# State part of a gated recurrence in 64-row tiles, with two output banks a chunk and a new hand-set order

## The chip, the cores and the metric

The kernel runs on one core of a Trainium2 chip. The metric is the device time of one execution in microseconds (us), lower is better. The engines are named as the profile names them: PE (matrix products; PEld is its weight load), DVE (vector), ACT (activation), POOL (general) and SP, whose queue issues the DMAs.

## The reference

Two stages follow each other. Per batch (4) and head (8), a recurrence over 768 steps with a 48 x 48 state, which is gated by alpha along its rows:

```python
for t in range(S):
    state = alpha[:, :, t, :, None] * state + np.einsum('bhd,bhe->bhde', k[:, :, t], v[:, :, t])
    y[:, :, t] = np.einsum('bhd,bhde->bhe', q[:, :, t], state)
```

Its output, with the heads side by side as 384 columns, is x. Then a mix over time of rank 32 and an MLP with a hidden width of 1536:

```python
xt = x.transpose(0, 2, 1)
h = xt @ U @ V
u = x + h.transpose(0, 2, 1)
ch = np.maximum(u @ w_ch1, 0.0) @ w_ch2
return u + ch
```

All inputs and the output are float32; the kernel computes its products in bfloat16 with float32 sums.

## The kernel before

**Chunks.** The 768 steps of a batch are cut into six chunks of 128. Inside a chunk the recurrence becomes products of matrices. `lt` is the logarithm of alpha, its cumulative sum over time comes from a product with a triangle of ones (L541 for whole chunks), and its exponentials `aa` and `ai` (L552, L551) scale q and k into `rkq` (L562). Scaled q and k are transposed to `kqt`, either on PE (L576) or, for the six chunks of batch 3, by a DMA that SP issues (L588). Their product gives the scores (L604), which a mask cuts to the past (L614, `pm`). The output of a chunk is y = scores x v (L671) + q x state (L666). The state is carried on: k x v of the chunk (L627) is added to the old state (L654, `sm`) and scaled by the chunk's total decay `tot` (L638, `st`).

**Two kinds of chunk.** In batch 0 and in the first four chunks of batch 1, loads come as pairs: one load holds four heads of two chunks (`stage_pair`). The other fourteen chunks are whole (`stage_gla`): chunks 4 and 5 of batch 1, and all of batches 2 and 3. The change is in the whole chunks. Heads stand there in pairs p = 0..3. In `kqt`, the even head of a pair lies in rows 0 to 47 and the odd one in rows 64 to 111. The score products use this: with `o = 64 * par` they take 48 rows each, in 64-row tiles of the PE array, even heads into one PSUM bank and odd heads into another. The state part of y does not: per pair it is one product over all 128 rows, which gives the 96 columns of both heads. For that the state must be zero where an even head's rows meet an odd head's columns. `tot` does it: it is made by two exponentials (L554), each with a bias from `off` of -30000 in one half of the rows, so that the total is 0 there. All of y of a chunk lies in one bank of 384 columns and is copied to `xb` by one instruction (L273 on ACT, L275 on DVE).

**After the recurrence.** `stage_mix` makes the mix of rank 32 (L686, L716) and the sum `ub` (L717), which is transposed to `uT` on PE (L736), or for batch 3 by DMA (L722). `mlp1` (L767) gives the hidden rows, ACT (L777) and DVE (L779) apply the maximum, `mlp2` (L793) gives the output, DVE adds `ub` (L799), and SP stores it (L802, L804). The 24 weight tiles are loaded once (L305) and cast by POOL or ACT.

**What sets the order.** Nothing is scheduled at run time or by the compiler. `P.add` lists every operation with the engines it may run on; the strings TABLE and SLOTS then say, operation by operation, which comes next, on which engine, and in which buffer of its pool. Each engine works through its instructions in that order. SP's queue does too: a load waits at its head until its buffer (one of 40 named `io`) has been read by the last user, and a store or a transpose by DMA until its data are made. The numbers of nanoseconds in `P.add` are a planner's estimates and do not act at run time. There are eight PSUM banks, given out by SLOTS, and four `kqt` buffers.

Of the kernel before, what the change touches and what calls it, by code (L numbers as in the profile page):

```python
# [16 lines left out]
A8SCcABASCzABQSETACePChACfAA+SCgACjDC1PC4AC3AC2AEVPEYABISA9SCiDCkPCmDClPBBSC5GEXADjADlPDnAEWACnDDmACoPCqDA-SCdGCrPCsDBDS  # L17
C0GDCPBCSC6GC7PBESCvPCpDC8PC+DDKACtPCuDCwPCxDDDDC9AC-PDADDBDABSAFGAGPAHDAJPAKADMPDPABKSCyDDEPDNADGPDFDDqGDsPBJSDpGDrPDtA
DuDDHPDJADZPBYSG2ABSSEaGBHSDLGDoAEcPDyPEeADIDBFSDQGDaPDbDDSPDUDDvPDwDBMSBLSDkGDzPD0DDxDG4PD8AD+PBRSEZGEbPEdDD3PDcPDdDDOA
BGSDRGDTPDVDG5AEAAD1PD2DBUSGfABOSEDGEfPEhDEgDD-AG7ABNSECGEBAG6ABTSBcSEUABPSD9GGhPGiAGjAGkAD4PELPBVSBWSGlGGmGBgSBXSGgGAAS  # L20
ADGBZSG8GAiSAjGAQSAeSAfGAgSAhGDWPDXDEiPD5PD7ABkSD6AEjPEkDEFPEEPEHAHNADYDEGDElPEMPENDAOSAPGARGEmPDfPAMSANGDePEnPEoADgPDiD
DhAAYSAZGBaSG9GAWSAUSAVGEIPEJDEKDHmAHPPHSAEPPGnPAXGASSATGHQABdSHTGBbSG3GEpAHRABiSBfSHOGAaSBhSBeSBoSAcSAkSBlSBjSAmSBpSAoS
BqSBmSGoPGqDGpDEOPAqSBnSHoPHrAEQPESDAuSAsSGuPGvDGwDEqPGrPGtDGsDERAErPHpAHqAHtGE8PE5PAwSAySEwPG+PHADE2PBrSEsAExPEyAE6PE7D
FFPE9PE+DA2SE3PEtPEzPFBPFCDFHPEuPFJPFGDE4AEvAE0PE1AF1PH-AFIDGyPF5PF3PF4DE-PFADFfPFgDF6AF2AFDPFhPFiAGxDFlPFmAFdPA4SACSFED
A0SFKDFLPFMAFNPFODG-PFjPFkAFeDA6SFVPFWAIBPICAFRPFSAHUGHBDHCPHDDAdGBsSGzPIEAIDAHFPFtPHGDHHDHIGIGGG0AAbAFuAHVPHXAG1AFnPHJP
B0SBwSBySB4SB8SFPPBuSBzSFQAHEDHKPHLAHMAHcPHdDHeDHsDIFAIVAFTPFUAFoAFrPFsAFpPHvPFqDHfDHxAHWPIXPIYAHuPHwDFvPFwDFZPFaDFzPF0D
HYAHiPHZPHbDHaDIZAAnAHyPHzDIHDFbPApAFcAHhPFxPFyAFXPHjPHkAHlAFYAHnGH1PH2DH3DH4DIIPIKAH6PAlGIaGIcPIbGIdPIfAIJPArGGTPIeAH7P
GNPH0DH8PH+AILDIMPH9DIODIgPIhDGBPIAGIPPH5GIRDF7PGZPHgGAzGAtAAvAAxAGOPINDITPF8PIQDIiDISGIWAIjPA5GGaPA3AGCPIUAAEGIkAIlPImD
GUPA1GA7AGbPGcDIvPIwDALGIzPI0DI1PI2DF9PF+DItPIuDGDPKLAGPPInPIpPIqDGEDKNPK0AI3PIxPIyDIoDKfAKOAI4AKPAKhPKjAKnGGVPGWDK2PK3A
LJAKlAJfPJgALeAKRAIrPIsDJRPJjPJSAJkDJdPJeAKiAKkAK6AKQAI5PJHPJIDJPPJQAJLPJMAI-PJAAK5AK4ALgPLkAJFPJGDJJPJKDLjABxSKmGKoPKqA  # L30
JTPJUDI6DKTGKVPJnPJoDLiALhABvSKMGBtSKSGKgAKUPJXPKWDKXDKbPKcDJlPLLPLMAJYDJbPJmAB9SB2SK8GKvPJBPK+PKwDKxDLAACASJcDJDPJEAB1S
KpPKrDGQDLOAK7GLNAJCAI9PI+ALPACESK9PK-DCMSNlAI7PI8DJVPJWALzAB3SK1GKsPKuDLBPLDDLCDKYPKZDJvPJNPJOAB6SLRGLTPLVAJhPL1PL2AL3A
B+SCCSB5SLHPLIANnPNqAB-SKtDLfALlGLnPKaDJwPL5GLQDCBSL4GLEPNrAKyPKzAJiAOIAB7SLKALpAGHPJZPGIPLSPLUAJaALFDLGGLmGKBPL6PL8DGJP
L7PGKDL9ALoPLqACNSCISCFSNoANsGLZPLaDJxPJyDNpACGSNtGKCPCKSCLSCQSCUSCDSLWPLXDL+PLrPKdPKeALYDLtDKDPJ7PLuPN2AN4PN5AJ8PJpPLbG
LsDLvDL-DLwGMADL0GOaAOcPOgAOfAOdACHSNmGN3GLcPN6ALdAN+GJ9PLxPLyDKEDMBPJqPNuSNvPNwDMCAMDPJrPOeAGMSNxDJ+DMEAN7AN8AOKPOMAAIG
MTPMUDMNPJ1PMLPMRPKGPMODJsDMMDCSSCRSOhGNyPNzDN0PMHPMIDKHPMFPMGDOsAOuPKIPMPPMQAMSDMJPMKDOOAMVPMWDKJDJ2PCWSOvAOLAMfPMXPMYD
J3PMjPM7POiGCYSO+AGFSCTSGGSPAPN1AONAObGGYSCJSCXSOtGCaSGSSKFSGLSN9GOwACPSOjSCVSOzGO0DOPDMkDMgDOxAOyAPBAPCAMbPMcDMpPMqAMlP
MmAJ4DNBPODPNDPMZPM-POEDMaAM8ANCACOSOQGNADM1PM2AOkPM5PNEDMxPMyAN-SM9PMhPM3PM4AJuSF-SMtPM6AMuAOJGOVPCZSPDGPEDOmDOlDOFDOWD
OXGMdPMeDM+AOnPOoDOpGNFPNGDMnPMoAMvPMiAOqPOrAOAPOBDO1SO2PO3DO4DOCDORSJ-SOSPOUDNHPMrPMsANRPMzPO5PO6DO7GOTDO8PO9ANSPGRSCbS
O-APFSJ5SPGPM0DPIDPHDGXSOGPOHANTPNUDOYPMwANIPPJPPKAOZAGASNJPNbPPLPNMPNcPPMAPPPPQDPSPPXPPNPPODPRSPYDPTDNdPNKDPUPPVDPWSNWP  # L40
# [101 lines left out]
def mm(*cols):  # L142
    return sum(max(c / 2.4 + 2.5, 25.0) for c in cols)
# [3 lines left out]
def kernel(  # L147
# [35 lines left out]
    QUEUE_U = (3,)  # L183
    P = Plan()
# [57 lines left out]
    off = const.tile([C, 2], FP32, name="off")  # L242
    nc.vector.memset(off, 0.0)
    nc.vector.memset(off[64:128, 0:1], -30000.0)
    nc.vector.memset(off[0:64, 1:2], -30000.0)
# [77 lines left out]
    def paired(b, c):  # L323
        return c // 2 < PAIRS[b]
# [22 lines left out]
    def xk(b, xb, c):  # L347
        return [(xb, c, 0), (xb, c, 1)] if paired(b, c) else [(xb, c)]
# [182 lines left out]
    def stage_gla(b, c, sprev, xb):  # L531
# [21 lines left out]
        for two in range(2 if c < NC - 1 else 0):  # L553
            P.add({"ACT": 100}, lambda e, two=two: nc.scalar.activation(  # L554
                tot().rearrange("p (a two) x -> p a (two x)", two=2)[:, :, two], cb()[:, DM : DM + HP], AF.Exp, bias=off[:, two : two + 1]
            ), r=[cb], w=[(tot, two)])
# [63 lines left out]
        if c < NC - 1:  # L620
# [15 lines left out]
            def f_st(e, src):  # L636
                eng = nc.gpsimd if e == "POOL" else nc.vector
                eng.tensor_tensor(  # L638
                    st().rearrange("p a (two d) -> p (a two) d", two=2),
                    src.rearrange("p (a d) -> p a d", d=D),  # L640
                    tot().to_broadcast([128, HP * 2, D]), op=ALU.mult,
                )

            if sprev is None:
                P.add({"DVE": 450}, lambda e: f_st(e, db()[:, 0:DM]), r=[db, (tot, 0), (tot, 1)], w=[st])
            else:
                sm = Buf(sms)
                W = DM // len(sprev)
                for n, (x, at0, key) in enumerate(sprev):

                    def f_add(e, n=n, x=x, at0=at0):
                        cs = slice(n * W, (n + 1) * W)
                        old = x()[:, at0 : at0 + HP // len(sprev), :].rearrange("p a d -> p (a d)")
                        nc.vector.tensor_tensor(sm()[:, cs], db()[:, cs], old, op=ALU.add)  # L654

                    P.add({"DVE": 460 if len(sprev) == 1 else 270}, f_add, r=[db, key], w=[(sm, n)])
                P.add({"POOL": 885, "DVE": 450}, lambda e: f_st(e, sm()), r=[(sm, n) for n in range(len(sprev))] + [(tot, 0), (tot, 1)], w=[st])

        yb = Buf(bank)

        def f_y(e):
            y = yb()[:, 0:DM]
            if sprev is not None:
                for p in range(HP):
                    x, at0, _ = sprev[p * len(sprev) // HP]
                    nc.tensor.matmul(  # L666
                        y[:, 2 * p * D : (2 * p + 2) * D], lhsT=qT()[:, p, :], rhs=x()[:, at0 + p % (HP // len(sprev)), :],
                        start=(p == 0), stop=False,
                    )
            for h in range(H):  # L670
                nc.tensor.matmul(  # L671
                    y[:, h * D : (h + 1) * D], lhsT=pm()[:, h // 2, h % 2, :], rhs=rv()[:, h, :],
                    start=(h == 0 and sprev is None), stop=(h == H - 1),
                )

        P.add({"PE": mm(*([2 * D] * 4 if sprev is not None else []), *[D] * 8)}, f_y, r=[qT, rv, (pm, 0), (pm, 1)] + [x[2] for x in sprev or ()], w=[yb])
        P.add({"ACT": 385, "DVE": 460}, lambda e: copy(e, xb()[:, c, :], yb()[:, 0:DM]), r=[yb], w=[(xb, c)])
        return st

    def stage_mix(b, xb, ub, uT):  # L680
# [17 lines left out]
        if b == 0:  # L698
# [15 lines left out]
        for c in range(NC):  # L714
# [13 lines left out]
            elif c % 2 == 1 and b > 0:  # L728
# [25 lines left out]
    def mlp1(b, uT, h1, tt):  # L754
        for jt in range(NJ):
            hb = Buf(bank)

            if b == 0:
# [99 lines left out]
```

## Time and profile before

| | us |
|---|---|
| median of 3 runs (lowest, highest) | 161.85 (159.73, 162.47) |
| the profiled execution, first to last instruction | 161.6 |
| busy: PE, PEld | 149.2, 98.7 |
| busy: DVE, ACT, POOL | 105.7, 90.8, 66.0 |
| L767 on PE (288 products) | 53.2 |
| L793 on PE (300 products) | 53.1 |
| bytes moved by DMA | 31.05 MB, 192 GB/s |

The span is what the times of all rows refer to: 0 is the first instruction of the program. Busy time of PE counts overlapping products once; a single product lasts longer (326 ns for 384 columns) than the distance from its start to the next one's. So PE's cost is read from start to start, not from the length of one. In rows of the timeline, the numbers are the start and the length of a group of like instructions that follow each other, and what stands in brackets is idle time ahead of it and what ended that. In rows of the grouped view they are busy time, the mean of one instruction in ns, and the idle time before with its releasers. "SPq" is SP's queue at work issuing a DMA.

### The profile page before, as it was taken

The page shows a single profiled execution, that of the slowest core. Times are in us where ns is not written, and L with a number is a line of the kernel's source. Part 1 is how long each engine was busy: PE and PEld are TensorE (multiplying, and loading weights), DVE is VectorE, ACT ScalarE, POOL GpSimd, SP SyncE. Part 2 cuts the span into 40 slices and gives each one's busy share as a digit, 9 for nine tenths or more (in the row PEclk, how much of TensorE's full clock was granted, in tenths as well). Part 3 has the DMA queues.
Part 4 walks back from the last instruction along what each step waited for, and adds up shares of the span by engine and source line. Part 5 has one row for each costly group of instructions (what it writes and reads, how often), then busy time and mean ns, then how long its engine had stood idle before and what let it go on. Part 6 is the DMA issues. An engine that isn't in the chain of part 4 may idle for free.

```text
span 161.6 us, 4518 instructions
## 1 busy us (share of the span) xinstructions
PE 149.2 (92%) x1728; PEld 98.7 (61%) x1728; DVE 105.7 (65%) x232; ACT 90.8 (56%) x234; POOL 66.0 (41%) x104
## 2 busy tenths in 40 slices
PE   0699897999999999999999999999889999999992
PEld 0586675665667656666676666755457565666662
DVE  6269897966697729559975959682898172334143
ACT  4765797557977645996897472845524301445000
POOL 8099756477667340283563664144622000000000
PEclk9999999999999999999999999999999999999999
DMA  4999995999999969889999899999992047840034
GB/s 125 289 312 315 248 250 150 268 336 253 285 229 279 293 130 209 176 176 203 207 195 215 160 189 198 195 226 204 146 204 67 0 81 172 262 146 0 0 129 163
DMA packets 96964, 31.05 MB, mean 192 GB/s; under 512 B 90640, under 2 KB 96912, under 8 KB 96944
## 3 DMA queue, kind: packets, MB, share of 16 engines
q1 hardware_dynamic: 96944, 30.78, 81.2%
q8 instruction: 13, 0.21, 0.5%
q14 instruction: 7, 0.06, 0.1%
HBM read 23.89 MB, written 4.72 MB: 177 GB/s over the span
## 4 chain that ended last, share of the span: by engine, by line
PE 54%; SPq 20%; DMA 14%; issue 4%; POOL 3%; DVE 2%; ACT 1%; POOLq 0%; DVEq 0%
PE ps L793 24%; PE ps L767 19%; SPq L332 13%; DMA io<-in_q_dram 5%; SPq L339 3%; DMA kqt<-rkq 3%; DMA io<-in_moe_w_ch_dram 2%; DMA io<-in_k_dram 2%; DMA io<-in_v_dram 2%; PE ps L576 2%; SPq L802 2%; SPq L305 2%; PE ps L604 1%; PE ps L716 1%; DVE pm L614 1%
## 5 line engine op out<-in xcount | busy, mean ns | idle before, releaser
L767 PE MATMUL ps<-uT,w_sb 128*128 128x384 bf16 x288 | 53.2, 326 | 0.4 <-POOL w_sb L277 0.4
L793 PE MATMUL ps<-w_sb,h1t 128*128 128x384 bf16 (+2 forms) x300 | 53.1, 319 | 0.0
L777 ACT ACTIVATE h1t<-ps 128x384 bf16<-128x384 f32 x61 | 27.6, 497 | 23.2 <-PE ps L767 23.1
L793 PEld LDWEIGHTS <-h1t 128*128 128x128 bf16 x300 | 27.1, 97 | 15.6 <-issue 0.8
L767 PEld LDWEIGHTS <-w_sb 128*128 128x128 bf16 x288 | 26.5, 98 | 16.4 <-POOL w_sb L277 1.2
L779 DVE TENSOR_SCALAR h1t<-ps 128x384 bf16<-128x384 f32 x35 | 18.6, 553 | 14.2 <-PE ps L767 14.2
L799 DVE TENSOR_TENSOR io<-ub,ps 128x384 f32<-128x384 bf16 (+2 forms) x25 | 13.3, 533 | 10.2 <-PE ps L793 10.0
L614 DVE TENSOR_TENSOR pm<-ps,maskc 128x512 bf16<-128x512 f32 x28 | 17.7, 682 | 1.1 <-PE ps L604 1.1
L562 POOL TENSOR_TENSOR rkq<-io,ai 128x384 bf16<-128x384 f32 x12 | 11.4, 949 | 13.8 <-DMA io<-in_k_dram 8.5
L717 DVE TENSOR_TENSOR ub<-xb,ps 128x384 bf16<-128x384 bf16 x24 | 12.4, 548 | 4.5 <-PE ps L716 4.3
L446 DVE TENSOR_TENSOR pm<-ps,maskp 128x512 bf16<-128x512 f32 x20 | 13.1, 683 | 2.4 <-PE ps L435 2.4
L562 POOL TENSOR_TENSOR rkq<-io,aa 128x384 bf16<-128x384 f32 x11 | 10.0, 912 | 9.8 <-ACT aa L552 8.4
L273 ACT CAST xb<-ps 128x192 bf16<-128x192 f32 (+1 forms) x27 | 10.3, 404 | 6.3 <-PE ps L671 4.9
L277 POOL CAST rv<-io 128x384 bf16<-128x384 f32 x18 | 9.4, 529 | 10.3 <-DMA io<-in_v_dram 9.3
L277 POOL CAST w_sb<-io 128x384 bf16<-128x384 f32 x16 | 8.0, 518 | 7.5 <-DMA io<-in_moe_w_ch_dram 7.5
L273 ACT COPY kqt<-ps 128x512 bf16<-128x512 bf16 x17 | 9.8, 610 | 1.9 <-PE ps L576 1.2
L275 DVE COPY kqt<-ps 128x512 bf16<-128x512 bf16 x19 | 7.8, 420 | 4.0 <-PE ps L576 2.2
L551 ACT ACTIVATE ai<-ps 128x384 bf16<-128x384 f32 x14 | 6.9, 498 | 5.5 <-PE ps L543 3.6
L411 PE MATMUL ps<-ident,rkq 128*128 128x128 bf16 x80 | 8.2, 237 | 1.6 <-DVE rkq L393 1.0
L393 POOL TENSOR_TENSOR rkq<-io,ai 128x384 bf16<-128x384 f32 x8 | 7.3, 910 | 5.8 <-DMA io<-in_k_dram 5.8
L638 POOL TENSOR_TENSOR st<-sm,tot 128x384 bf16<-128x384 f32 x7 | 5.8, 829 | 6.6 <-DVE sm L654 6.6
L393 POOL TENSOR_TENSOR rkq<-io,aa 128x384 bf16<-128x384 f32 x9 | 8.2, 910 | 0.6 <-DMA io<-in_q_dram 0.3
(114 smaller groups left out, 217.1 us busy)
## 6 DMA issues: line engine op xcount, KB each, us to landing
io<-in_alpha_dram SPq DMA_DIRECT2D x24, 192.0 KB, 3.8
io<-in_q_dram SPq DMA_DIRECT2D x24, 192.0 KB, 3.7
io<-in_k_dram SPq DMA_DIRECT2D x24, 192.0 KB, 3.7
io<-in_v_dram SPq DMA_DIRECT2D x24, 192.0 KB, 3.8
io<-in_moe_w_ch_dram SPq DMA_DIRECT2D x24, 192.0 KB, 3.9
out_dram<-io SPq DMA_DIRECT2D x13, 192.0 KB, 1.9
out_dram<-io SPq DMA_DIRECT2D x20, 96.0 KB, 2.3
out_dram<-io SPq DMA_DIRECT2D x1, 120.0 KB, 1.7
```

The costliest lines, as they stand in the source:

```text
L273: nc.scalar.copy(dst, src)
L277: nc.gpsimd.tensor_copy(dst, src)
L332: lambda e: nc.sync.dma_start(t().rearrange("p (h j) d -> p h (j d)", j=2), src[b, hs, sl, :].rearrange("h (p j) d -> p h (j d)", j=2)),
L393: eng.tensor_tensor(jh(dst()[:, :, 0:D]), raw(a), jh(x()), op=ALU.mult)
L446: nc.vector.tensor_tensor(dst, s2, maskp.to_broadcast([C, 2, 2, C]), op=ALU.mult)
L562: eng.tensor_tensor(dst()[:, :, 0:D], a(), x(), op=ALU.mult)
L614: nc.vector.tensor_tensor(pm()[:, :, par, :], s2, maskc.to_broadcast([C, HP, C]), op=ALU.mult)
L767: nc.tensor.matmul(hb()[:, 0:TW], lhsT=w1_sb[:, ct, jt * 128 : (jt + 1) * 128], rhs=u_half(uT, ct, tt, b in QUEUE_U), start=(ct == 0), sto ...
L777: nc.scalar.activation(dst, hb()[:, 0:TW], AF.Relu)
L779: nc.vector.tensor_scalar_max(dst, hb()[:, 0:TW], 0.0)
L793: nc.tensor.matmul(hb()[:, 0 : hi - lo], lhsT=h1()[:, jt, c * C : (c + 1) * C], rhs=w2_sb[:, jt, lo:hi], start=(jt == 0), stop=(jt == NJ - 1),
L799: P.add({"DVE": 468}, lambda e, hb=hb, lo=lo, hi=hi: nc.vector.tensor_tensor(flat(ou)[:, lo:hi], ub()[:, c, lo:hi], hb()[:, 0 : hi - lo], ...
```

## The change

For whole chunks:

- The state part of y is its own step `f_ys`. Per pair of heads it has two products of 48 rows and 48 columns in place of one of 128 rows and 96 columns, the even head in the upper 64-row tile and the odd head in the lower one.
- y lies in two banks, one for even and one for odd heads, with 192 columns used in each. Each is copied to `xb` by an instruction of its own, with a target in blocks of 48 columns.
- `tot` is made by one exponential of four columns; `off` and its three fills are gone. The state's blocks between heads of a pair are no longer set to 0, and nothing reads them. The scaling (`f_st`) spreads one factor over 96 columns.
- The order of all operations, the engine of those that may run on several, and the buffers are new (TABLE and SLOTS), for the whole program. `SUM_U` only gives the test for batch 0 a name.

```diff
-        for two in range(2 if c < NC - 1 else 0):
-            P.add({"ACT": 100}, lambda e, two=two: nc.scalar.activation(
-                tot().rearrange("p (a two) x -> p a (two x)", two=2)[:, :, two], cb()[:, DM : DM + HP], AF.Exp, bias=off[:, two : two + 1]
-            ), r=[cb], w=[(tot, two)])
+        if c < NC - 1:
+            P.add({"ACT": 100}, lambda e: nc.scalar.activation(tot()[:, 0:HP, 0], cb()[:, DM : DM + HP], AF.Exp), r=[cb], w=[tot])
...
-        yb = Buf(bank)
+        yb = Buf(bank), Buf(bank)
+
+        def f_ys(e):
+            for p in range(HP):
+                x, at0, _ = sprev[p * len(sprev) // HP]
+                for par in range(2):
+                    o = 64 * par
+                    nc.tensor.matmul(
+                        yb[par]()[:, p * D : (p + 1) * D],
+                        lhsT=qT()[o : o + D, p, :], rhs=x()[o : o + D, at0 + p % (HP // len(sprev)), par * D : (par + 1) * D],
+                        start=(p == 0), stop=False, skip_group_check=True,
+                    )
 
         def f_y(e):
-            y = yb()[:, 0:DM]
-            if sprev is not None:
+            for par in range(2):
                 for p in range(HP):
-                    x, at0, _ = sprev[p * len(sprev) // HP]
                     nc.tensor.matmul(
-                        y[:, 2 * p * D : (2 * p + 2) * D], lhsT=qT()[:, p, :], rhs=x()[:, at0 + p % (HP // len(sprev)), :],
-                        start=(p == 0), stop=False,
+                        yb[par]()[:, p * D : (p + 1) * D], lhsT=pm()[:, p, par, :], rhs=rv()[:, 2 * p + par, :],
+                        start=(p == 0 and sprev is None), stop=(p == HP - 1), skip_group_check=True,
                     )
...
+        if sprev is not None:
+            P.add({"PE": mm(*[D] * 4)}, f_ys, r=[qT] + [x[2] for x in sprev], w=[yb[0], yb[1]], mode="R")
+        P.add({"PE": mm(*[D] * 8)}, f_y, r=[rv, (pm, 0), (pm, 1)], w=[yb[0], yb[1]])
+        for par in range(2):
+            P.add(
+                {"ACT": 250, "DVE": 265},
+                lambda e, par=par: copy(
+                    e, xb()[:, c, :].rearrange("t (p two d) -> t p two d", two=2, d=D)[:, :, par], yb[par]()[:, 0 : HP * D].rearrange("t (p d) -> t p d", d=D)
+                ),
+                r=[yb[par]], w=[(xb, c, par)],
+            )
```

By engine, PE has 48 products more (1776 for 1728), 16 instructions are gone from ACT and DVE has 16 more; POOL and SP have as many as before. In SP's queue the order of loads, transposes and stores is another one: the first load is alpha of batch 1, chunk 4 (a whole chunk) in place of batch 0, chunk 0.

More of the change, by code (lines that the diff above doesn't have):

```diff
@@ L347, in xk @@
     def xk(b, xb, c):
[L348 removed]
+        return [(xb, c, 0), (xb, c, 1)]
     def stage_pair(b, u, sprev, xb):
@@ L656, in stage_gla @@
                     P.add({"DVE": 460 if len(sprev) == 1 else 270}, f_add, r=[db, key], w=[(sm, n)])
-                P.add({"POOL": 885, "DVE": 450}, lambda e: f_st(e, sm()), r=[(sm, n) for n in range(len(sprev))] + [(tot, 0), (tot, 1)], w=[st])
-        yb = Buf(bank)
+                P.add({"POOL": 885, "DVE": 450}, lambda e: f_st(e, sm()), r=[(sm, n) for n in range(len(sprev))] + [tot], w=[st])
+        yb = Buf(bank), Buf(bank)
[9 more added lines that the diff above has]
+                    )
@@ L727, in stage_mix @@
                     )
-            elif c % 2 == 1 and b > 0:
+            elif c % 2 == 1 and b not in SUM_U:
                 ub2 = Buf(bank)
```

93 lines of the change are left out of this document (40 added, 53 removed).

## The prediction

> **What bounds the kernel now.** I read the page's summary first, then windows by stage, then the chain of waits, then the timelines of PE and of SP's queue.
>
> ```profile
> span 161.6 us, 4518 instructions
> ...
> PE   0699897999999999999999999999889999999992
> ...
> DMA  4999995999999969889999899999992047840034
> ```
>
> ```profile
> core 0: us, PE busy (x) PEld busy (x) DVE busy (x) ACT busy (x) POOL busy (x), PEclk, DMA share, GB/s
> 0.00:31.40 31.40, 24.02 (x460) 18.41 (x461) 23.26 (x71) 21.01 (x58) 19.78 (x38) 1.00 0.91 241
> 31.40:60.00 28.60, 27.93 (x360) 17.69 (x358) 19.51 (x42) 20.18 (x51) 18.20 (x31) 1.00 0.99 262
> 60.00:105.00 45.00, 44.93 (x493) 30.41 (x491) 34.62 (x67) 32.29 (x87) 20.26 (x26) 1.00 0.97 193
> 105.00:120.00 15.00, 13.70 (x123) 8.18 (x122) 11.00 (x21) 6.80 (x17) 6.98 (x8) 1.00 1.08 195
> ```
>
> The reader is to see two limits of nearly the same size. PE is full from 31.4 us on, except between 105 and 120 us, where it lacks 1.3 us. The DMA engines are full until about 120 us. No other engine is near its limit in any stage (DVE, the next, has 34.6 of 45 us). The chain says which limit counts where:
>
> ```profile
> 27.58 3.94 DMA io<-in_moe_w_ch_dram
> 32.14 0.50 PE ps L767 x2
> ...
> 114.06 4.30 DMA kqt<-rkq
> 118.41 0.40 PE ps L604 x8
> ...
> 135.20 11.70 PE ps L767 x72
> ...
> 158.73 0.30 DVE io L799
> ```
>
> The MLP starts when its fourth weight tile is there, and the last stop of PE is for a transposed tile of batch 3 at 118.41. From there PE never stops. So the end is the landing of a late transfer plus the PE work that stands behind it, plus 161.6 - 158.7 = 2.9 us of output. A matmul of 384 columns is 11.70 / 72 = 0.1625 us.
>
> **The state part of y.** Row by row on PE, one group between two full-array groups, and the same for y:
>
> ```profile
> 77.19 0.81 PE L767 MATMUL ps<-uT,w_sb 128*128 128x384 bf16 x4
> 77.94 0.84 PE L604 MATMUL ps<-kqt 48*128 48x128 bf16 x24
> 78.71 0.82 PE L793 MATMUL ps<-w_sb,h1t 128*128 128x384 bf16 x4
> 79.37 0.65 PE L767 MATMUL ps<-uT,w_sb 128*128 128x384 bf16 x3
> ```
>
> ```profile
> 55.41 0.33 PE L666 MATMUL ps<-st,kqt 128*128 128x96 bf16 x4
> 55.58 0.36 PE L671 MATMUL ps<-rv,pm 128*128 128x48 bf16 x8
> 55.79 0.81 PE L793 MATMUL ps<-w_sb,h1t 128*128 128x384 bf16 x4
> ```
>
> Read from start to start. The state part (L666) takes 55.58 - 55.41 = 0.17 us; the other eight products (L671) 0.21, so 26 ns for a product of 48 columns. The 24 products in 64-row tiles take 0.77 us, 0.064 for each pair with the changes of shape in it; in turn, at the 55 ns that 128 columns take at the same rate, they would take 1.3. So two row halves run side by side. New, the state part is 4 pairs of 48 columns, 4 x 0.026 = 0.10 us. Twelve whole chunks have a state: 12 x (0.17 - 0.10) = 0.84 us off PE.
>
> Against it: four L767 should take 0.65 and take 0.75 before the tiled group, while four L793 take 0.66 where no shape changes. Entering costs 0.10; 12 pairs at 55 ns are 0.66 of the 0.77, so leaving costs 0.10 too. In PE's order of instructions the shape changes 58 times before and 70 times after, because the new groups stand partly alone: 12 x 0.10 = 1.2 us onto PE. The sum is +0.4 us; were every new group next to another tiled one it would be -0.84, and with the pairs in turn +1.6. I take +0.4. [...]
>
> **Totals, evictions and the second bank.**
>
> ```profile
> L554 ACT ACTIVATE tot<-ps,off 128x4 f32<-128x4 f32 x22 | 5.4, 278 | 0.7 <-POOL st L638 0.7
> L273 ACT CAST xb<-ps 128x384 bf16<-128x384 f32 x13 | 6.2, 482 | 4.9 <-PE ps L671 4.9
> L273 ACT CAST xb<-ps 128x192 bf16<-128x192 f32 x14 | 4.2, 332 | 1.3 <-PE ps L518 1.2
> L275 DVE CAST xb<-ps 128x192 bf16<-128x192 f32 x6 | 2.1, 353 | 0.6 <-PE ps L518 0.6
> L562 POOL TENSOR_TENSOR rkq<-io,ai 128x384 bf16<-128x384 f32 x12 | 11.4, 949 | 13.8 <-DMA io<-in_k_dram 8.5 <-ACT tot L554 2.6 <-ACT ai L551 2.6
> L638 POOL TENSOR_TENSOR st<-sm,tot 128x384 bf16<-128x384 f32 x7 | 5.8, 829 | 6.6 <-DVE sm L654 6.6
> L534 ACT ACTIVATE lt<-io 128x384 bf16<-128x384 f32 x14 | 7.4, 531 | 0.8 <-DMA io<-in_alpha_dram 0.7
> ```
>
> Eleven of the 22 small exponentials go: -11 x 0.278 = -3.1 us of ACT. Fourteen evictions become 28 of half the width: +14 x (2 x 0.332 - 0.482) = +2.5 us (on DVE 0.353 each). In sum nothing; PE's full work hides both, and if it did not, one chunk's y would come 0.2 us later. The strided target of the new evictions is not in the trace: between the 192-wide row and the 384-wide one, +0 to +2.1 us, taken as 0, since the source holds the same 192 elements. The state's scaling keeps its 384 elements, two more of them on POOL: +1.7 us, in its idle time. A second bank for y, with eight banks in all, can make PE wait for an eviction. The largest such wait before is 0.43 us (next fence), so 0 to +0.5; nothing below 0 comes of it. I take 0, as y's banks are emptied sooner in two halves.
>
> **The order.** It is new on all queues. What counts is SP's order against PE's. Counting DMAs along SP's queue and PE instructions in program order, I take for the n-th DMA the issue time of the n-th before, add the landing and the first step after it, and add the PE work that the new order puts behind the instruction that needs it.
>
> ```profile
> 28.53 1.80 SPq L305 DMA_DIRECT2D io<-in_moe_w_ch_dram  x3
> 69.39 0.66 SPq L339 DMA_DIRECT2D io<-in_alpha_dram  x1
> 80.59 0.76 SPq L339 DMA_DIRECT2D io<-in_v_dram  x1
> 96.10 1.31 SPq L339 DMA_DIRECT2D io<-in_alpha_dram  x1
> 107.22 0.59 SPq L339 DMA_DIRECT2D io<-in_k_dram  x1
> ```
>
> ```profile
> io<-in_alpha_dram SPq DMA_DIRECT2D x24, 192.0 KB, 3.8
> io<-in_k_dram SPq DMA_DIRECT2D x24, 192.0 KB, 3.7
> kqt<-rkq SPq DMA_TRANSPOSE x6, 3.8
> ```
>
> These are the 41st to 43rd, the 90th, 101st, 117th and 130th DMA of SP's queue; the first 90 DMAs are in both orders 40 loads of paired chunks, 22 of whole chunks, 24 weight tiles and 4 small ones, so the same bytes. PE work is counted at 0.1625 us for 384 columns, in proportion for fewer, 26 ns at the least, tiled pairs as one, plus 0.10 for each change of shape.
>
> First the method on the kernel before: behind the tiled group at 118.41 stand 39.5 us and 5 changes, so PE ends at 158.4; it ends at 158.7. I add the 0.3 below.
>
> - Start: alpha of a whole chunk is now loaded first and its logarithm is made first; the second load and one ACT step (0.53) later, PE's first matmul comes some 0.5 us after 3.99 (row below). The three memsets that go were done within that. DMA sets the next 30 us, so I count 0, at most +0.5.
> - Start of the MLP: its third weight tile, which completes the first group, is now the 42nd DMA, not the 39th: issued at about 29.4 (the second of three from 28.53) for 27.6, so 34.0 us for 32.1. But the new order puts more of batch 1 ahead of it, and 117.8 us and 34 changes stand behind: 34.0 + 121.2 = 155.2. No limit.
> - Alpha of batch 2, chunk 1 is the 90th DMA (before, the 79th): 69.4 + 3.8 + 0.53 = 73.7. Its cumulative sum has 415 matmuls of 384 columns (67.4) and 15.0 of smaller work behind it, with 21 changes: 73.7 + 82.5 + 2.1 = 158.3.
> - k of batch 2, chunk 4 is the 101st: 80.6 + 3.7 + 0.95 for the product on POOL = 85.2; behind it 71.5 and 17 changes: 158.4.
> - k of batch 3, chunk 0 is the 117th: 96.1 + 3.7 + 0.95 = 100.8; 55.9 and 10 changes: 157.7.
> - k of batch 3, chunk 5 is the 130th (before the 135th, with five stores more ahead): 107.2 + 3.7 + 0.95 + 3.8 for the transpose = 115.7; 39.0 and 5 changes: 155.2.
>
> ```profile
> 3.99 0.48 PE L371 MATMUL ps<-lt,upto 128*128 128x384 bf16 x1 [3.99 <-DVE off L243]
> ...
> 113.91 0.33 PE L627 MATMUL ps<-rv,rkq 128*128 128x96 bf16 x4 [0.43 <-ACT h1t L777]
> ...
> 118.41 0.40 PE L604 MATMUL ps<-kqt 48*128 48x128 bf16 x8 [0.47 <-DMA kqt<-rkq]
> ```
>
> So the late stop goes: the last transposes have 3 us to spare. What is late next is batch 2's loads, at 70 to 85 us, and they give the same end. The sum: 158.4 + 0.3 + 2.9 = 161.6, the time before. Two limits within 0.1 us of each other leave room for small slips, +0.2. The span was 161.6 and the median of the runs 161.85, +0.25. Forecast: 162.0 us, no change that can be measured (2% or 3.2 us, about what a measurement of this kernel tells from none; its own runs go from 159.73 to 162.47). Its own range is 160.6 (y's changes of shape free, -1.2, and no slip) to 163.0 (evictions and bank waits on the path, 0.5 each).
>
> **The rivals.**
>
> *Faster: batch 2's loads come early enough.* SP stood still for buffers in the kernel before:
>
> ```profile
> SPq L305 <- POOL w_sb L277: 3.2, 2, 2.6
> ```
>
> If the new order has no such stop, everything behind it comes up to 3.2 us sooner, and PE's own work, 155.2 + 0.3 from the start of the MLP, becomes the limit: 155.5 + 2.9 + 0.25 = 158.6. For it: PE had only 1.3 us idle after 31.4 us and DMA fell just short. Against it: the DMA row is at 9 throughout, so that a stop of SP is mostly covered by transfers in flight. Chance 0.13.
>
> *Slower: SP is held by batch 1's buffers.* The new order loads batch 2 and the last weight tiles (72nd to 91st DMA) into buffers that hold k and q of batch 1 until POOL has multiplied them, where the order before used from the 77th to the 84th almost only buffers of weight tiles already cast. POOL does each product in 0.95 us and was busy 18.2 of 28.6 us there. If POOL is behind, the load stands at the head of SP's queue, and all that follow wait with it. One such stop cost 2.6 us before and two 3.2. As the limits of batch 2 have no slack, it goes to the end one for one from the first 0.1 us on: 162.0 + 3.2 = 165.2, and with one us more it is plainly past 2%. Chance 0.16.
>
> *The change does not do what it says:* the two row halves of the state part run in turn after all, 12 x 0.10 = +1.2: 163.2. Against it is the row of the tiled scores. Chance 0.05, within 2%.
>
> **How the numbers follow.** Forecast 0.66, faster 0.13, slower 0.16, in turn 0.05. Of the faster case most lies just past 2% and some within, as does the slower: faster by over 2% 0.12, within 2% 0.71, slower 0.17. The range leaves out a tenth at each end: 158.9 to 165.2.
>
> **What would show it.** A state group standing alone between full-array groups takes about 0.30 us from start to start with its two changes, and one next to tiled scores 0.10. The small exponentials are 11. PE loses some 2 us more than before between 40 and 75 us, waiting for the logarithm of alpha of batch 2, and stops no more than half a microsecond between 105 and 125. The 90th DMA is issued near 69.4. The forecast is wrong if that DMA is issued more than 3 us away from there, or if PE stops for a late transpose or an eviction in the last 40 us.

## The result, and the profile after

The changed kernel takes 168.19 us (median of 4 runs, 166.88 to 169.52) against 161.37 for the kernel before beside it (4 runs, 159.73 to 162.47). The ratio is 1.0425, with a 95% interval of 1.0350 to 1.0499: slower. The forecast was 162.0, the range 158.9 to 165.2; the time lies above both.

The page's summary of the kernel after:

```profile
span 167.1 us, 4594 instructions
...
PE   0589999999869999999899999999999999999991
...
DMA  5999999999999979999999999989970066840153
```

The windows by stage:

```profile
core 0: us, PE busy (x) PEld busy (x) DVE busy (x) ACT busy (x) POOL busy (x), PEclk, DMA share, GB/s
0.00:31.40 31.40, 24.05 (x434) 18.32 (x434) 20.45 (x61) 20.76 (x55) 21.22 (x39) 1.00 1.02 229
31.40:60.00 28.60, 26.47 (x380) 16.84 (x377) 23.16 (x53) 20.48 (x52) 17.38 (x29) 1.00 0.99 240
60.00:105.00 45.00, 43.99 (x476) 29.09 (x474) 33.05 (x64) 26.93 (x73) 16.71 (x23) 1.00 1.14 199
105.00:120.00 15.00, 14.70 (x143) 9.44 (x141) 13.97 (x28) 7.57 (x19) 8.97 (x12) 1.00 0.98 170
```

The late stop is gone, as forecast: between 105 and 120 us PE is busy 14.70 of 15 us, where it was 13.70. The time is lost earlier. From 31.4 to 60 us PE lacks 2.1 us (before 0.7), from 60 to 105 another 1.0 (before 0.1), and in the first 31.4 us it has done 434 products where it had done 460. The chain of waits (start, length, what) has a weight tile and then loads of batch 1 and 2 in these places, and the loads of batch 1 and 2 are long (4.4 to 5.5 us):

```profile
30.40 2.98 DMA io<-in_moe_w_ch_dram
...
33.92 5.54 DMA io<-in_q_dram
...
42.00 5.53 DMA io<-in_q_dram
...
74.23 4.40 DMA io<-in_k_dram
...
78.79 0.91 POOL rkq L558
...
80.34 4.57 DMA io<-in_q_dram
```

What the forecast had not reckoned with is in the DMA view. Here is the same stretch, 6 to 20 us, of the kernel before and of the changed kernel, in this order; in the second line stand packets, MB, and their time as a share of 16 engines:

```profile
DMA packets 10826, 4.13 MB, mean 295 GB/s; under 512 B 10793, under 2 KB 10793, under 8 KB 10825
...
q1 hardware_dynamic: 10825, 4.11, 109.6%
```

```profile
DMA packets 9102, 3.49 MB, mean 249 GB/s; under 512 B 9069, under 2 KB 9069, under 8 KB 9101
...
q1 hardware_dynamic: 9101, 3.47, 120.4%
```

Both kernels load paired chunks there. A packet is the unit that the DMA view counts; here it has 384 bytes, but for a few. Per packet, before took 14 us x 16 engines x 1.096 / 10825 = 22.7 ns, and after 14 x 16 x 1.204 / 9101 = 29.6 ns. The DMA engines are no less full than before and move 16% less. On the page, the median from issue to landing rises for alpha from 3.8 to 4.2 us and for k from 3.7 to 4.5:

```profile
io<-in_alpha_dram SPq DMA_DIRECT2D x24, 192.0 KB, 4.2
...
io<-in_k_dram SPq DMA_DIRECT2D x24, 192.0 KB, 4.5
```

Neither profile says what makes a packet take 29.6 ns in place of 22.7. So the question was what in the change does.

### The profile page after: what moved, and what is told of

Same layout as the page of the kernel before. It is cut to its first block, busy times and chain, and to the rows that moved or that the text cites. A ratio compares the mean times of both kernels' runs of the same rounds, so it can differ in the third digit from the quotient of the medians.

```text
span 167.1 us, 4594 instructions
## 1 busy us (share of the span) xinstructions
PE 152.8 (91%) x1776; PEld 100.6 (60%) x1776; DVE 112.7 (67%) x248; ACT 84.9 (51%) x218; POOL 66.1 (40%) x104
## 4 chain that ended last, share of the span: by engine, by line
PE 52%; SPq 17%; DMA 16%; DVE 4%; POOL 3%; issue 3%; ACT 2%; DVEq 0%; POOLq 0%
PE ps L798 23%; PE ps L772 18%; SPq L330 15%; DMA io<-in_q_dram 9%; DMA io<-in_moe_w_ch_dram 4%; DMA io<-in_k_dram 3%; PE ps L667 2%; PE ps L721 2%; PE ps L600 2%; POOL rkq L558 1%; PE ps L741 1%; POOL rkq L391 1%; PE ps L658 1%; DVE h1t L784 1%; DVE io L804 1%
## 5 line engine op out<-in xcount | busy, mean ns | idle before, releaser
L782 ACT ACTIVATE h1t<-ps 128x384 bf16<-128x384 f32 x54 | 25.6, 492 | 25.8 <-PE ps L772 25.4
L784 DVE TENSOR_SCALAR h1t<-ps 128x384 bf16<-128x384 f32 x42 | 22.1, 550 | 15.7 <-PE ps L772 15.3
L558 POOL TENSOR_TENSOR rkq<-io,ai 128x384 bf16<-128x384 f32 x9 | 8.2, 913 | 16.7 <-DMA io<-in_q_dram 7.6
L271 ACT CAST xb<-ps 128x192 bf16<-128x192 f32 x28 | 8.2, 327 | 11.5 <-PE ps L667 10.1
L558 POOL TENSOR_TENSOR rkq<-io,aa 128x384 bf16<-128x384 f32 x11 | 10.7, 972 | 5.5 <-DMA io<-in_q_dram 2.9
L634 POOL TENSOR_TENSOR st<-sm,tot 128x384 bf16<-128x384 f32 x9 | 7.8, 861 | 10.5 <-DVE sm L646 9.9
L532 ACT ACTIVATE lt<-io 128x384 bf16<-128x384 f32 x14 | 7.4, 528 | 7.1 <-DMA io<-in_alpha_dram 7.1
L275 POOL CAST rv<-io 128x384 bf16<-128x384 f32 x14 | 7.1, 504 | 9.6 <-DMA io<-in_v_dram 8.5
L271 ACT COPY kqt<-ps 128x512 bf16<-128x512 bf16 x15 | 8.8, 592 | 2.9 <-PE ps L572 2.1
L369 PE MATMUL ps<-lt,upto 128*128 128x384 bf16 x10 | 4.3, 432 | 6.3 <-ACT lt L360 6.3
L391 POOL TENSOR_TENSOR rkq<-io,aa 128x384 bf16<-128x384 f32 x10 | 9.1, 913 | 1.7 <-DMA io<-in_q_dram 1.1
```

Source lines behind the costliest of these rows:

```text
L271: nc.scalar.copy(dst, src)
L275: nc.gpsimd.tensor_copy(dst, src)
L558: eng.tensor_tensor(dst()[:, :, 0:D], a(), x(), op=ALU.mult)
L782: nc.scalar.activation(dst, hb()[:, 0:TW], AF.Relu)
L784: nc.vector.tensor_scalar_max(dst, hb()[:, 0:TW], 0.0)
```

## The experiments

### First: the order or the arithmetic?

Two theories were open. O: the new order is slower. A: the new arithmetic is (changes of shape, copies, banks). Each was tried alone.

**The changed arithmetic in the order of before.**

```diff
 # the changed kernel
 TABLE = """
-BkSH-ABASBISCzAC1PA8SDjADlPDoABCSBDSC0GC3AIBPC2AC4AIEACcADnABBSICACePCfAC5DDCPCgADDDC7PC9DC6GC8PChAC+DC-PDADDBDA-SABSAFG
...
+A8SCcABASCzABQSETACePChACfAA+SCgACjDC1PC4AC3AC2AEVPEYABISA9SCiDCkPCmDClPBBSC5GEXADjADlPDnAEWACnDDmACoPCqDA-SCdGCrPCsDBDS
...
```

> The changed arithmetic (state part by heads in 64-row tiles, two banks, one exponential for the totals) with the instructions in the order of the kernel before; around chunks 4 of batch 1 and 0 of batch 3 some fourteen instructions stand a few places later, because all eight banks are taken there. If the new order makes the time (theory O): 161 to 162.5 us, ratio 0.995 to 1.01. If the new arithmetic does, by tile switches, evictions or the second bank (theory A): 166 to 168 us, ratio 1.03 to 1.04. If both do, each about half: 164 to 165. In the trace theory O expects the 384-byte pair loads to land every 0.58 to 0.60 us as in before, and a state group of four pairs to cost 0.2 to 0.3 us against 0.17.

Measured: 171.83 us (170.91 to 172.38), ratio 1.0694 [1.0632, 1.0756]. That is slower than the whole change and outside what either theory had named. Its packets took 29.2 ns (14 x 16 x 1.247 / 9567), though its order of loads is that of before.

**The arithmetic of before in the changed order.**

```diff
 # the kernel before
 TABLE = """
-A8SCcABASCzABQSETACePChACfAA+SCgACjDC1PC4AC3AC2AEVPEYABISA9SCiDCkPCmDClPBBSC5GEXADjADlPDnAEWACnDDmACoPCqDA-SCdGCrPCsDBDS
...
+BkSH-ABASBISCzAC1PA8SDjADlPDoABCSBDSC0GC3AIBPC2AC4AIEAIFACcADnABBSICACePCfAC5DDCPCgADDDC7PC9DC6GC8PChAC+DC-PDADDBDA-SABS
...
```

> The arithmetic of the kernel before (state part over 128 rows in one bank, two biased exponentials, one copy out) in the order of the changed kernel; the state part stands with the rest of y, at the later of its two places. Theory O (the order): 167 to 169 us, ratio 1.035 to 1.05, and the pair loads land every 0.72 to 0.75 us. Theory A (the arithmetic): 161 to 163 us. If the slow landings of the changed kernel's profile were of that one execution and not of its order, they land every 0.58 to 0.60 us here, whatever the time is.

Measured: 164.75 us (163.50 to 165.21), ratio 1.0268 [1.0208, 1.0329], between the two theories. Its packets took 22.7 ns (14 x 16 x 1.103 / 10871). So the packets follow the code, not the order, and theory O, which had them follow the order, is out as far as they go. But the kernel has fast packets and is still slower than before, so some of its time comes from something else; this was not taken apart.

**The first 20 us.** Two more kernels ran beside these, on the late start of PE and on its slower products there (four products of 128 columns last 0.59 to 0.63 us until 20.3 us, and 0.39 at 22.5).

```diff
 # the changed kernel, in SP's, ACT's and PE's order (as a sketch; TABLE and SLOTS have it in code)
-alpha 1.4, alpha 0.1, alpha 0.3, alpha 0.0, ...
+alpha 0.1, alpha 0.3, alpha 0.0, ..., alpha 1.2, alpha 1.4, ...
```

> The changed kernel, with alpha of chunk 4 of batch 1 loaded and worked on (logarithm, sum, three exponentials) not first of all but behind alpha of its chunk 2, some 37 loads later, near its place in the kernel before. If the late start of TensorE (5.18 us against 3.99) and the work on a chunk that is used 40 us later set the first 30 us, MLP 1 starts 1 to 2 us earlier and the time is 166 to 167. If the landings of the loads set them (the third weight tile is the 42nd load with or without it), MLP 1 starts as before and the time is 168 within 0.5.

Measured: 169.74 us (169.14 to 170.34), ratio 1.0569 [1.0511, 1.0628]. PE began at 4.08 us instead of 5.18 and the MLP still began at 39.32 instead of 36.69. The early load is not the cause; putting it back made things worse, and why was not followed up.

```diff
 # the changed kernel; ++K is ten matmuls of zeros, each ++C two
 TABLE = """
-BkSH-ABASBISCzAC1PA8SDjADlPDoABCSBDSC0GC3AIBPC2AC4AIEACcADnABBSICACePCfAC5DDCPCgADDDC7PC9DC6GC8PChAC+DC-PDADDBDA-SABSAFG
...
+++KBkSH-ABASBISCzAC1PA8SDjADlP++CDoABCSBDSC0GC3AIBP++CC2AC4AIEACcADnABBSICACeP++CCfAC5DDCPCgADDDC7PC9DC6GC8PChAC+DC-PDAD
...
```

> The changed kernel with sixteen matmuls of zeros that nothing reads, of 512 columns into a bank that is free there: ten ahead of the first matmul, two each in three gaps of the first 13 us, so that TensorE is at full rate from the start (it took 107 ns for 128 columns until 21 us in the changed kernel, until 13 us in before). If half rate on TensorE sets the first stage: MLP 1 starts 2 to 3 us earlier and the time is 165 to 166. If the loads set it: no change, 168 within 0.5.

Measured: 167.94 us (167.33 to 170.25), ratio 1.0445 [1.0382, 1.0507], which cannot be told from the changed kernel's own 1.0425. The MLP began at 36.37 us.

### Second: the place of the buffers

In all four kernels with the changed code a packet took 29.0 to 29.6 ns, in the two with the old code 22.7, whatever the order. From 6 to 20 us all of them load paired chunks; what the code changes for such a load is where its target is allocated. `off` was a tile of 8 bytes a partition, which takes 32 in the compiled program, and it stood just ahead of the 40 `io` buffers that all loads write. With it the compiled program has them begin at byte 95232 of a partition, a multiple of 256. Without it they begin at 95200, 224 past such a multiple. A buffer is 1536 bytes, 6 x 256, so all 40 keep that distance. Theory S: this shift slows the packets, and with them the kernel.

**The shift taken back.**

```diff
 # the changed kernel
+    const.tile([C, 2], FP32, name="pad")
     io = Pool(slots("io", 40, [C, H, D], FP32))
```

> The changed kernel with one unused tile of 8 bytes allocated where the tile off was, and nothing else: no instruction is added or taken away. Off took 32 bytes of each partition ahead of the 40 io buffers; without it they begin at byte 95200 (224 past a multiple of 256, 32 past one of 64) and not at 95232 (a multiple of both), as do all tiles behind them. Theory S (the shift of the buffers slows the packets of the loads, 29 to 31 ns for 384 bytes against 22): they take 22 ns again, the pair loads land every 0.58 to 0.60 us, MLP 1 starts 2 to 3 us earlier, and the time is 161 to 165 us. Theory A (the matmuls, copies and totals as such): 168 within 1, and the packets as in the changed kernel.

Measured: 162.80 us (162.64 to 163.23), ratio 1.0041 [0.9983, 1.0100]: no difference from before. One line that adds no instruction takes away 5.4 us (168.19 to 162.80; the two did not run side by side, and by the ratios to before it is 3.8%). The DMA view, 6 to 20 us:

```profile
q1 hardware_dynamic: 10777, 4.09, 109.6%
```

That is 22.8 ns a packet, and the medians from issue to landing are back at 3.8 us for alpha and k. The loads of whole chunks, with packets of 192 bytes for the most part, gain too. From 70 to 80 and 80 to 90 us together, first the changed kernel, then this one:

```profile
q1 hardware_dynamic: 17981, 3.93, 119.4%
```

```profile
q1 hardware_dynamic: 19206, 3.83, 98.6%
```

20 x 16 x 1.194 / 17981 = 21.2 ns against 20 x 16 x 0.986 / 19206 = 16.4.

**The kernel before, shifted.**

```diff
 # the kernel before
+    const.tile([C, 2], FP32, name="pad")
     io = Pool(slots("io", 40, [C, H, D], FP32))
```

> The kernel before with one unused tile of 8 bytes more ahead of the io buffers, so that they begin at 95264 (32 past a multiple of 64 and of 256). No instruction is changed. Theory S: packets of 384 bytes take 28 to 31 ns in the first 20 us, and the time is 167 to 171 us, ratio 1.04 to 1.06. Theory A: 160 to 162, ratio 1.00.

Measured: 166.78 us (165.86 to 168.35), ratio 1.0264 [1.0188, 1.0339]; packets 14 x 16 x 1.224 / 9381 = 29.2 ns (the trace is of its longest run, 168.35 us). The kernel before, with not one instruction changed, gets slow packets and becomes slower; the interval lies above 1, though it reaches below 2%. That is less than was expected (1.04 to 1.06), and why was not measured.

**The changed arithmetic in the order of before, shift taken back.**

```diff
 # the kernel e1_maths_alone
+    const.tile([C, 2], FP32, name="pad")
     io = Pool(slots("io", 40, [C, H, D], FP32))
```

> The changed arithmetic in the order of the kernel before (as in e1_maths_alone, 171.83 us), with the unused 8 bytes ahead of the io buffers. Theory S: 161 to 164 us, and what is left over the kernel before is the price of the arithmetic and of the few instructions moved. Theory A: 171 within 1.

Measured: 170.08 us (170.04 to 170.52), ratio 1.0492 [1.0432, 1.0553]. This is a miss: theory S had 161 to 164. The packets are fast again (14 x 16 x 1.087 / 10639 = 22.9 ns) and the MLP begins at 31.51 us (31.44 in before); the time is lost later. The timeline of PE, with idle time and releaser in brackets, and the windows:

```profile
83.77 0.32 PE L541 MATMUL ps<-lt,ut_ones 128*128 128x384 bf16 x1 [0.88 <-ACT xb L273]
...
97.40 0.27 PE L660 MATMUL ps<-st,kqt 48*128 48x48 bf16 x8 [0.35 <-ACT xb L273]
...
98.66 0.19 PE L660 MATMUL ps<-st,kqt 48*128 48x48 bf16 x1 [0.69 <-DVE xb L275]
99.11 0.31 PE L660 MATMUL ps<-st,kqt 48*128 48x48 bf16 x7 [0.26 <-DVE io L806]
...
99.68 1.46 PE L800 MATMUL ps<-w_sb,h1t 128*128 128x384 bf16 x4
101.07 0.61 PE L602 MATMUL ps<-kqt 48*128 48x128 bf16 x8
...
102.37 0.82 PE L800 MATMUL ps<-w_sb,h1t 128*128 128x384 bf16 x4
103.03 0.33 PE L541 MATMUL ps<-lt,ut_ones 128*128 128x384 bf16 x1
...
123.70 0.83 PE L602 MATMUL ps<-kqt 48*128 48x128 bf16 x23 [0.37 <-ACT xb L273]
...
132.53 0.81 PE L800 MATMUL ps<-w_sb,h1t 128*128 128x384 bf16 x4 [0.32 <-ACT xb L273]
```

```profile
60.00:97.00 37.00, 35.99 (x386) 23.87 (x385) 26.50 (x50) 25.19 (x68) 16.57 (x21) 1.00 0.94 186
97.00:105.00 8.00, 6.70 (x71) 3.60 (x71) 4.17 (x9) 2.73 (x9) 3.74 (x6) 0.79 0.87 183
105.00:120.00 15.00, 14.46 (x122) 9.10 (x121) 11.87 (x23) 7.18 (x19) 4.65 (x6) 1.00 1.08 193
```

Here PE waits for y's banks to be emptied: 0.88 + 0.35 + 0.69 + 0.37 + 0.32 = 2.6 us at instructions that need a bank, with `xb`, the copy out of y's banks, as the releaser. From 97 to 105 us, in and behind the run of stops at 97 to 99, PE's granted clock (the column behind POOL's) is 0.79 on the mean, where it is 1.00 from 60 to 97 and from 105 to 120; four products of 384 columns take 1.39 us from start to start at 99.68 and 0.66 at 102.37. So 8 x 0.21 = 1.7 us of its rate are lost as well (an estimate from the 0.79). These make some 4 of the 7.7 us over before. All stops of PE behind 31.4 us come to 4.7 us, among them 1.09 for a weight tile at 38.28, where before has 1.8; counted so, 2.9 + 1.7 = 4.6 us of the 7.7 are found and the rest is open. So the second bank has a price in an order that has no free bank for it; in the changed order no stop of PE has `xb` as its releaser.

**Only the io buffers back in place.**

```diff
 # the changed kernel
+    const.tile([C, 2], FP32, name="pad")
     io = Pool(slots("io", 40, [C, H, D], FP32))
+    const.tile([C, 2], FP32, name="pad2")
```

> The changed kernel with two unused tiles of 8 bytes, one ahead of the io buffers and one behind them: the io buffers lie at multiples of 64 as before, all tiles behind them 32 bytes past one. If only the loads suffer from the shift: as e5_after_pad within 0.7 us. If matmul, vector or scalar operands behind them suffer too: nearer to the changed kernel's 168, by at least 1.5 us.

Measured: 163.51 us (162.45 to 163.58), ratio 1.0066 [1.0001, 1.0130], the same as e5_after_pad within the intervals. The operands of the engines behind the buffers lie 32 bytes off and it costs nothing that can be told. It is the `io` buffers that count. The engines read them too, but that is not what costs: POOL's product from k takes 913 ns in the changed kernel and 916 in e5_after_pad, the one from q 972 in both.

**How far off is off?**

```diff
 # the changed kernel
+    const.tile([C, 2], FP32, name="pad")
+    const.tile([C, 2], FP32, name="pad2")
+    const.tile([C, 2], FP32, name="pad3")
     io = Pool(slots("io", 40, [C, H, D], FP32))
```

> The changed kernel with three unused tiles of 8 bytes ahead of the io buffers, so that these begin at 95296: a multiple of 64, but 64 past a multiple of 256. If what matters is a start at a multiple of 64 bytes: packets of 384 bytes take 22 ns, and the time is 162 to 164 us, as e5_after_pad. If the distance to a multiple of 256 matters: 24 to 27 ns or more, and 165 to 168 us. [...]

Measured: 165.81 us (165.23 to 167.15), ratio 1.0237 [1.0153, 1.0320]; packets 14 x 16 x 1.216 / 9374 = 29.1 ns. For the packets of 384 bytes a multiple of 64 is not enough. For the whole chunks it is. Here are 70 to 90 us, first e9_shift64, then e6_before_shift, which is off by 32:

```profile
q1 hardware_dynamic: 20078, 4.27, 102.5%
```

```profile
q1 hardware_dynamic: 19315, 3.65, 115.9%
```

That is 20 x 16 x 1.025 / 20078 = 16.3 ns, as good as in place, against 20 x 16 x 1.159 / 19315 = 19.2.

| io begins past a multiple of 256 by | ns a packet, 6 to 20 us (384 bytes) | ns a packet, 70 to 90 us (mostly 192 bytes) | kernels |
|---|---|---|---|
| 0 | 22.4 to 22.9 | 15.4 to 16.4 | before, e2, e5, e8; 6 to 20 us also e7, e10, e11, e12 |
| 32 | 29.2 | 19.2 | e6 |
| 64 | 29.1 | 16.3 | e9 |
| 224 | 29.0 to 29.6 | 19.9 to 21.3 | after, e1; 6 to 20 us also e3, e4 |

So the distance of the buffers alone does not give the time: at 64, packets of 384 bytes take 29.1 ns for 22.4 to 22.9, and the window with mostly 192 bytes has 16.3 as in place. The author's reading is that it counts where the packets start; no run varied that apart from the buffers. A packet of 192 bytes starts in a buffer at 0, 64, 128 or 192 past a multiple of 256, and a shift by 64 gives the same four starts again; a packet of 384 bytes starts at 0 or 128, and after the shift at 64 or 192.

For 384 bytes the runs show one step of some 30% at any of the three distances (29.0 to 29.6 ns for 22.4 to 22.9), and in the windows with mostly 192 bytes one of 17 to 38% at 32 and 224 (19.2 to 21.3 for 15.4 to 16.4). What makes the step is not shown. At distance 0, half of the 384-byte packets start at 128 past a multiple of 256, and the whole is not slow; whether a start at 128 is as good as one at 256 was not told apart.

### Third: what is left

**Warm-up with the loads at full pace.**

```diff
 # the kernel e4_warm
+    const.tile([C, 2], FP32, name="pad")
     io = Pool(slots("io", 40, [C, H, D], FP32))
```

> The changed kernel with the unused 8 bytes ahead of the io buffers and the sixteen matmuls of zeros of e4_warm. With the loads at full pace, half rate on TensorE (until 18 us in e5_after_pad) may now be what sets the first stage: then 160 to 161.5 us, ratio 0.985 to 0.995, a version that beats the kernel before. If the loads still set it: 162.8 within 0.7, as e5_after_pad.

Measured: 162.99 us (161.67 to 165.76, 10 runs), ratio 1.0081 [1.0040, 1.0122]. The MLP begins at 34.01 us, 1.1 earlier than in e5_after_pad, and the time is no shorter. No version that beats the kernel before was found.

**Totals and state part apart.** The first of these is the kernel e2_order_alone once more, the second has the totals of before in the changed kernel.

> The kernel e2_order_alone once more (arithmetic of before, order of the changed kernel, io buffers at a multiple of 64), for a comparison on one chip with e12_totals_old. By the prediction's sum the new state part and totals save TensorE 0.84 us of matmuls and cost it up to 1.2 us of changes of tile shape: this kernel within 1 us of e12_totals_old. If the second copy, the second bank or the changes of shape cost more than that: e12_totals_old is slower by over 1 us. If the eleven or twelve exponentials matter, they do so in both alike.

```diff
 # the changed kernel
+    off = const.tile([C, 2], FP32, name="off")
...
-        if c < NC - 1:
-            P.add({"ACT": 100}, lambda e: nc.scalar.activation(tot()[:, 0:HP, 0], cb()[:, DM : DM + HP], AF.Exp), r=[cb], w=[tot])
+        for two in range(2 if c < NC - 1 else 0):
+            P.add({"ACT": 100}, lambda e, two=two: nc.scalar.activation(
+                tot().rearrange("p (a two) x -> p a (two x)", two=2)[:, :, two], cb()[:, DM : DM + HP], AF.Exp, bias=off[:, two : two + 1]
+            ), r=[cb], w=[(tot, two)])
...
```

> The changed kernel with only the totals undone: two biased exponentials a chunk as in before, the second behind the first on ScalarE, and the tile off with them, so that the io buffers begin at a multiple of 64 again; state part and order stay as changed. By theory S the eleven small exponentials come back and the time falls all the same, to e5_after_pad's 162.8 within 1 us, since what the edit to the totals cost was the 32 bytes and not the exponentials. By a theory in which the totals' arithmetic matters: slower than the changed kernel, over 168.

Measured: 164.29 us (163.94 to 164.75), ratio 1.0156 [1.0086, 1.0226], and 164.01 us (163.08 to 164.80), ratio 1.0135 [1.0053, 1.0218]. Side by side, the old and the new state part differ by 0.3 us with ranges that overlap: no difference. And with the eleven exponentials put back, the changed kernel is 4.2 us faster than without them (168.19), because `off` comes back with them (a packet of 384 bytes takes 22.4 ns, 29.6 without). Whether they cost something for themselves (164.01 against e5_after_pad's 162.80, not side by side, with intervals that overlap) stays open.

## Why the prediction was wrong

**The step that failed** is in the part on the order: "I take for the n-th DMA the issue time of the n-th before, add the landing", with "so the same bytes" as its reason. The bytes are the same; the time for them is not (29.6 ns for a packet of 384 bytes, 22.7 before). The edit was in the text: `off` and its three fills go. The prediction counted the fills ("The three memsets that go were done within that") and not the 32 bytes of each partition that go with the tile. The sums then used landings of 3.7 and 3.8 us from before, where k measured 4.5 and alpha 4.2, and issue times that came late for the same reason. SP's queue in the changed kernel, at the 41st and 42nd, the 90th, 101st, 117th and 130th DMA:

```profile
30.95 0.91 SPq L303 DMA_DIRECT2D io<-in_moe_w_ch_dram  x2
...
71.72 0.38 SPq L337 DMA_DIRECT2D io<-in_alpha_dram  x1
...
82.42 0.94 SPq L337 DMA_DIRECT2D io<-in_k_dram  x1
...
98.85 0.95 SPq L337 DMA_DIRECT2D io<-in_k_dram  x1
...
114.09 0.69 SPq L337 DMA_DIRECT2D io<-in_k_dram  x1
```

and in e5_after_pad, the same order with the buffers in place:

```profile
26.89 1.05 SPq L305 DMA_DIRECT2D io<-in_moe_w_ch_dram  x2
...
66.17 0.39 SPq L339 DMA_DIRECT2D io<-in_alpha_dram  x1
...
76.01 0.75 SPq L339 DMA_DIRECT2D io<-in_k_dram  x1
...
92.83 0.70 SPq L339 DMA_DIRECT2D io<-in_k_dram  x1
...
108.06 0.70 SPq L339 DMA_DIRECT2D io<-in_k_dram  x1
```

The forecast had 69.4, 80.6, 96.1 and 107.2 for the last four. With packets of 29.6 ns they come 1.8 to 6.9 us later than that. With packets of 22.8 ns the first three come 3.2 to 4.6 earlier, and the last 0.9 later. As the prediction said of batch 2's loads, there was no slack to take it in: the loads of batch 1 and 2 are on the chain after, and PE stops for what is made from them.

```profile
48.62 0.40 PE L572 MATMUL ps<-ident,rkq 128*128 128x128 bf16 x4 [1.34 <-POOL rkq L558]
...
82.84 0.33 PE L623 MATMUL ps<-rv,rkq 128*128 128x96 bf16 x4 [0.51 <-ACT rv L271]
```

**The sign named for it was too blunt.** The forecast was to be wrong if the 90th DMA is issued more than 3 us away from 69.4. It was issued 2.3 away, and the forecast was wrong all the same. Other signs came out as told: 11 small exponentials, and no stop of PE over 0.30 us between 105 and 125 us. Between 40 and 75 us PE stopped for 1.8 us (before 0.3), near the 2 us named, but 1.34 of it for batch 1's product on POOL and not for the logarithm of batch 2's alpha: a size hit with another wait behind it. The time of a packet in a window, which would have shown it at once, was not among the signs.

**The rest of the sum, with the buffers in place.** e5_after_pad took 162.80 us against the 162.0 forecast, in part by errors that cancel:

- *State part.* Right. In the changed kernel, between full-array products: the eight products of y at 54.63 take 0.30 to the next start where they take 0.21 at 93.85, and the group behind them 0.20, so 0.09 for entering, and 0.10 each for its products and for leaving if they are split as the prediction did, 0.29 in all for the 0.30 forecast. Next to scores it takes 0.11 (93.20 to 93.31).

```profile
54.63 0.36 PE L667 MATMUL ps<-rv,pm 128*128 128x48 bf16 x8
54.93 0.27 PE L658 MATMUL ps<-st,kqt 48*128 48x48 bf16 x8
55.13 0.66 PE L772 MATMUL ps<-uT,w_sb 128*128 128x384 bf16 x3
...
93.20 0.27 PE L658 MATMUL ps<-st,kqt 48*128 48x48 bf16 x8
93.31 0.61 PE L600 MATMUL ps<-kqt 48*128 48x128 bf16 x16
93.85 0.37 PE L667 MATMUL ps<-rv,pm 128*128 128x48 bf16 x8
94.06 0.33 PE L623 MATMUL ps<-rv,rkq 128*128 128x96 bf16 x4
```

- *Totals and copies.* Right: eleven exponentials remain, shorter than those with a bias (182 ns for 278). The 28 copies of 192 columns on ACT, of both kinds of chunk, take 327 ns (before 332); the 17 from 56 us on, which are all of whole chunks with the strided target, have a median of 319. Both rows are of the changed kernel. The bank for the odd heads made no stop on PE in the changed order; e7_maths_pad shows 2.6 us where the order doesn't provide for it, far over the 0 to 0.5 that the prediction allowed.

```profile
L271 ACT CAST xb<-ps 128x192 bf16<-128x192 f32 x28 | 8.2, 327 | 11.5 <-PE ps L667 10.1 <-PE ps L516 1.3
...
L552 ACT ACTIVATE tot<-ps 128x4 f32<-128x4 f32 x11 | 2.0, 182 | 2.5 <-PE ps L541 2.5
```

- *The limits of batch 2* were not the end: in e5_after_pad its loads came earlier than assumed and PE was never idle from 31.4 to 60 us and 0.1 us from 60 to 105. This is what the "faster" rival had as its condition, with PE's own work behind the start of the MLP as the limit. But it gave no gain. The MLP began at 35.14 us and not at 34.0, though its third weight tile was issued 2 us earlier than forecast (at 27.4 for 29.4): the chain up to there has no load after the first alpha, so that work on PE, ACT and POOL set the start, and not DMA as the prediction had it. PE's first product came at 5.56 us, 1.6 after that of before, for at most 0.5 forecast.

```profile
31.40:60.00 28.60, 28.60 (x381) 19.05 (x379) 23.70 (x54) 22.15 (x56) 16.62 (x29) 1.00 1.01 241
60.00:105.00 45.00, 44.88 (x489) 29.94 (x488) 35.86 (x71) 26.55 (x72) 19.91 (x27) 1.00 0.97 198
```

- *From span to time* the prediction added 0.25 us, span 161.6 to median 161.85. That was mis-sized. In every run with both numbers, the time is 1.7 to 2.1 above the span (168.88 at 167.1 after, 162.84 at 161.1 in e5_after_pad, 161.26 at 159.5 in a run of before). So the execution of before whose trace was shown had a time of about 163.4 (an estimate from its span of 161.6), 1.5 above the median, and the span forecast, 162.0 - 0.25 = 161.75, would be a time of about 163.5. The span of e5_after_pad is 0.65 below that forecast; its time is 0.8 above the time forecast.

**The rivals.** The slower one named the right side and a wrong mechanism. It had SP held by batch 1's buffers until POOL has multiplied them. SP was so held in the changed kernel, 3.1 us in five waits ahead of loads of whole chunks (first row below). With the buffers in place it was held as long, 2.3 us ahead of weight tiles and 0.8 ahead of whole chunks (second and third row), and PE did not stop for it: the order and the buffers' use are the same in both. That the row halves run in turn is out by the row at 93.20 (eight products of 48 columns in 0.11 us, where eight at 26 ns in turn would be 0.21).

```profile
SPq L337 <- POOL rkq L558: 3.1, 5, 1.6
```

```profile
SPq L305 <- POOL rkq L560: 2.3, 3, 1.1
...
SPq L339 <- POOL rkq L560: 0.8, 3, 0.4
```

## What to carry to other kernels

Here a tile of 8 bytes that went moved the 40 buffers behind it by 32 bytes, and a packet of 384 bytes took 29.6 ns for 22.7; so list the addresses of the buffers that DMAs write, before and after, as part of reading a diff. When a kernel loads in packets of a few hundred bytes, compare the time of a packet in the same window of both traces before looking for a cause in the order. An arithmetic that needs one more bank is to be judged in an order that has one to give: PE stopped for 2.6 us with `xb` as releaser in e7_maths_pad, and no stop in the changed order has that releaser.

## What the runs showed of the hardware that was not expected

- A shift of the load buffers in SBUF by 32 or 64 bytes changed the time of their packets. Packets of 384 bytes took 22.4 to 22.9 ns where the buffers begin at a multiple of 256 bytes, and 29.0 to 29.6 where they begin 32, 64 or 224 past one. Windows with mostly packets of 192 bytes had 15.4 to 16.4 ns at 0, 16.3 at 64, 19.2 at 32 and 19.9 to 21.3 at 224. In the full kernel that is worth 2 to 4% (e5_after_pad's 1.0041 against 1.0237 at 64 past and 1.0425 at 224 past; 1.0264 for the kernel before at 32 past).
- Operands of the engines moved by 32 bytes, with the `io` buffers left in place, cost nothing that could be told (1.0066 [1.0001, 1.0130] against 1.0041 [0.9983, 1.0100]).
- Stops of PE of 0.35, 0.69 and 0.26 us within two us stand just ahead of four products of 384 columns that take 1.39 us (0.66 at 102.37), and the granted clock is 0.79 on the mean from 97 to 105 us, in a kernel that has 1.00 from 60 to 97 and from 105 to 120 (e7_maths_pad); that the stops set it off is not shown.
